# The second layer of an attention-plus-MLP kernel by Strassen's identity, for eight chunks of nine

## The chip, the cores and the metric

The kernel runs on one core of a Trainium2 chip. The metric is the device time of the program in microseconds: before the change the median of three runs is 338.12 us (336.65, 338.12 and 338.40). Five engines work beside each other, each through its own instructions in order: TensorE (PE) with its weight loads (PEld), VectorE (DVE), ScalarE (ACT), GpSimd (POOL), and SyncE (SP), which here only issues transfers. PE writes to PSUM, eight banks of 512 fp32 columns for each of 128 partitions; DVE and ACT carry results from there to SBUF.

## What is computed

Causal attention over 8 batches ("sequences" below) of 8 heads, 576 positions and 64 columns, with 16 beacon keys and values that every query sees, and then an MLP over the 4608 rows of 512 that come out.

```python
def _attn_ref(q, k, v, beacon_k, beacon_v):
    B, H, S, D = q.shape                       # 8, 8, 576, 64
    k_all = np.concatenate([beacon_k, k], axis=2)
    v_all = np.concatenate([beacon_v, v], axis=2)
    ...
    a = np.exp(scores)
    a /= a.sum(-1, keepdims=True) + 1e-09
    return np.matmul(a, v_all)

def _moe_ref(x, w_in, w_out):                  # x 4608x512, w_in 512x2048, w_out 2048x512
    h = x @ w_in
    g = np.maximum(0.01 * h, h)
    return (g @ w_out).astype(np.float32)
```

Inputs and output are fp32; the matmuls take bf16.

## The kernel before

**Attention.** The work goes by pairs of heads, `g` from 0 to 31, four pairs to a sequence. Queries and keys come through POOL's queue, as bf16. For the first eight pairs PE transposes them (`t_q`); for the later ones they are loaded in natural order (`load_natural`, pool `natpool`) and turned by transposing transfers that SP issues (`turn_pair`). Scores go to PSUM; later pairs pack them into blocks of three 1024-column tiles (`stretch`), of which the first takes two buffers of the pool `ps_one` and the others the pool `ps_sc`. ACT takes the exponential into `aT`, POOL sets the masked triangles to zero. `value` multiplies by the values in two halves (12 and 18 matmuls of 65 columns); DVE divides by the row sums (a reciprocal, L380, and a product, L381) and leaves `x_nat`. `x_transposes` (PE and a copy, L398) or `x_turn` (two transposing transfers from SP) put it into `xT`, the activations of all 4608 tokens with model columns on partitions.

**MLP.** Tokens go in nine chunks of 512. `moe1(i, fc)` (an "up") is four matmuls of 512 columns for one of 16 blocks of 128 hidden columns, then a Prelu on ACT (L431) into `gT`, one of two buffers. The second layer ("downs") goes by tiles of 128 tokens: `moe2_part` does 16 matmuls, in four quarters, with `gT` as weights and `w_out_sb` moving, into one PSUM buffer that is held through the four quarters; then DVE copies it to `osb` (L484, two buffers) and SP stores it (L485). Only the very last tile is split into 384 and 128 columns, the latter copied and stored by ACT.

**PSUM.** `ps_sc` has two buffers of two banks. `ps_one` has four buffers of one bank, shared by ups, downs, values, transposes and the first tile of each score block.

**Order.** The order of instructions on all five engines is the program's own. The first eight pairs follow a list of steps written as strings (`run`: `s` scores, `v` values, `u` up, `d` down, `x` finish and so on). Behind it a list of events with due times in units of pairs is walked through; between events `fill` puts in ups and downs so that they are spread evenly over the time. A chunk's ups come as soon as all its tokens are in `xT`, and its downs after all its ups. The last downs stand alone.

SP's queue holds, in order, the transposes of queries and keys, those of `x_nat`, and the output stores. POOL's holds the masks and the loads of q, k and v.

Of the kernel before, what the change touches and what calls it, by code (L numbers as in the profile page):

```python
# [15 lines left out]
def kernel(  # L16
# [11 lines left out]
    nc = tc.nc  # L28
# [31 lines left out]
    NA, NK = 4, 8  # L60
    LAID = 2 * NPAIR
# [15 lines left out]
    qkpool = ctx.enter_context(tc.tile_pool(name="qkpool", bufs=2))  # L77
    natpool = ctx.enter_context(tc.tile_pool(name="natpool", bufs=6))
    headpool = ctx.enter_context(tc.tile_pool(name="headpool", bufs=2))
    gpool = ctx.enter_context(tc.tile_pool(name="gpool", bufs=2))  # L80
    opool = ctx.enter_context(tc.tile_pool(name="opool", bufs=2))
# [10 lines left out]
    w_out_r = moe_w_out.rearrange("(c p e) d -> p c (e d)", p=128, e=2)  # L92

# [4 lines left out]
    xT = singles.tile([128, NJ, NTOK], BF16, name="xT")  # L98
# [5 lines left out]
    first_k = singles.tile([RP, 2, RI, D], FP32, name="first_k")  # L104
    k_nat0 = singles.tile([RP, RI, 2, D], BF16, name="k_nat0")
# [30 lines left out]
    def raw_of(b, grp):  # L136
        if (b, grp) not in qk_raw:
            qk_raw[b, grp] = (
                qkpool.tile([128, 2, RI, D], BF16, name="q_raw"),
                qkpool.tile([128, 2, RI, D], BF16, name="k_raw"),  # L140
            )
        return qk_raw[b, grp]
# [244 lines left out]

    def x_transposes(g, copy):
        b, hp = divmod(g, NPAIR)
        x_nat, _ = xs.pop(g)  # L390
        ps = ps_one.tile([128, 1024], BF16, name="tp", tag="one")
        for t, (q0, rows) in enumerate(QT):
            nc.tensor.transpose(
                ps[:, q0 : q0 + rows],
                x_nat[0:rows, t].rearrange("p e d -> p (e d)"),
                ident[0:rows, 0:rows],
            )
        copy(out=xT[:, hp, b * S : (b + 1) * S], in_=ps[:, 0:S])  # L398

    def x_turn(g):  # L400
        b, hp = divmod(g, NPAIR)
        x_nat, _ = xs.pop(g)
        t1 = NKB if b < B - 1 else NKB - 1
        dst = xT[:, hp, b * S : b * S + 112 + (t1 - 1) * 128]
        nc.sync.dma_start_transpose(
            out=dst[:, 112:].rearrange("c (t r) -> c t r", r=128),
            in_=x_nat[:, 1:t1].rearrange("r t e d -> r (t e d)"),
        )
        if t1 < NKB:
            nc.sync.dma_start_transpose(  # L410
                out=xT[:, hp, NTOK - 80 :], in_=x_nat[0:80, t1].rearrange("r e d -> r (e d)")
            )
        nc.sync.dma_start_transpose(  # L413
            out=dst[:, 0:112], in_=x_nat[0:112, 0].rearrange("r e d -> r (e d)")
        )
# [3 lines left out]
    def moe1(i, fc):  # L419
        if i not in gT:  # L420
            gT[i] = gpool.tile([128, NF, 512], BF16, name="gT")
        acc = ps_one.tile([128, 512], FP32, name="acc", tag="one")
        for j in range(NJ):
            nc.tensor.matmul(  # L424
                out=acc,
                lhsT=w_in_cols(fc, j),
                rhs=xT[:, j, i * 512 : (i + 1) * 512],
                start=(j == 0),
                stop=(j == NJ - 1),
            )  # L430
        nc.scalar.activation(out=gT[i][:, fc, :], in_=acc, func=AF.Prelu, alpha=0.01)  # L431

    early = {}

    def moe1_early(n, j):
        if j == 0:
            early[n] = ps_sc.tile([128, 2, 512], FP32, name="sc", tag="sc")
            if 0 not in gT:
                gT[0] = gpool.tile([128, NF, 512], BF16, name="gT")
        for e in range(2):  # L440
            fc = 2 * n + e
            nc.tensor.matmul(
                out=early[n][:, e],
                lhsT=w_in_cols(fc, j),
                rhs=xT[:, j, 0:512],
                start=(j == 0),
                stop=(j == NJ - 1),
            )
        if j == NJ - 1:
            nc.scalar.activation(  # L450
                out=gT[0][:, 2 * n : 2 * n + 2, :], in_=early[n], func=AF.Prelu, alpha=0.01
            )
            done1[0] += 2

    acc2 = [None]

    def moe2(i, t, quarter):
        t0 = i * 512 + t * 128
        if t0 + 128 < NTOK:
            moe2_part(i, t, quarter, quarter + 1, 0, DM, nc.vector.tensor_copy, nc.sync)  # L460
            return
        n = 3 * DM // 4
        if quarter < 3:
            moe2_part(i, t, 4 * quarter // 3, 4 * (quarter + 1) // 3, 0, n, nc.vector.tensor_copy, nc.sync)
        else:
            moe2_part(i, t, 0, 4, n, DM, nc.scalar.copy, nc.scalar)

    def moe2_part(i, t, q0, q1, lo, hi, copy, eng):
        if q0 == 0:
            acc2[0] = ps_one.tile([128, 512], FP32, name="acc", tag="one")  # L470
        acc = acc2[0][:, 0 : hi - lo]
        for fc in range(q0 * 4, q1 * 4):
            nc.tensor.matmul(  # L473
                out=acc,
                lhsT=gT[i][:, fc, t * 128 : (t + 1) * 128],
                rhs=w_out_sb[:, fc, lo:hi],
                start=(fc == 0),
                stop=(fc == NF - 1),
            )
        if q1 < 4:  # L480
            return
        t0 = i * 512 + t * 128
        osb = opool.tile([128, hi - lo], FP32, name="osb" if lo == 0 and hi == DM else f"osb{lo}")
        copy(out=osb, in_=acc)  # L484
        eng.dma_start(out=out[t0 : t0 + 128, lo:hi], in_=osb)  # L485

    done1, done2, ready, turn, first_down, held = [0], [0], [0], [0], [0], [0]

    def fill():
        i1, fc = divmod(done1[0], NF)  # L490
        i2, n2 = divmod(done2[0], NF)
        can1 = i1 < ready[0] and (i1 < 2 or i2 > i1 - 2)
        can2 = i2 < NCH and i2 < i1 and done1[0] >= first_down[0]
        if held[0] and can2:
            held[0] -= 1
            down()
        elif can1 and (turn[0] == 0 or not can2):
            up()
        elif can2:
            down()  # L500
        return can1 or can2

    def up():
        i1, fc = divmod(done1[0], NF)
        assert i1 < ready[0]
        moe1(i1, fc)
        done1[0] += 1
        turn[0] = 1

    def down():  # L510
        i2, n2 = divmod(done2[0], NF)
        moe2(i2, n2 // 4, n2 % 4)
        done2[0] += 1
        turn[0] = 0
# [40 lines left out]
    def run(steps):  # L555
        for step in steps.split():
# [27 lines left out]
            elif op == "P":  # L584
                moe1_early(*a)
# [8 lines left out]
            elif op == "o":  # L594
                load_w_out(a[0])
            else:
# [12 lines left out]
    with order:  # L609
# [23 lines left out]
        run("m7.1 m7.2 N9.1 u b8.2 b9.2 b10.2 b11.2 x6 v7.0 T9 v7.1 d d d N10.0 N10.1 d V2.0 V2.1 x7 T10")  # L633
# [22 lines left out]
        def has_down():  # L656
            return done2[0] // NF < done1[0] // NF
# [28 lines left out]
        for at, _, what, args in events:  # L686
            while w + 2 < len(ends) and at > ends[w + 1]:
                w, d0 = w + 1, done1[0] + done2[0]
            todo = 2 * NF * ready[0] - KEPT - d0
# [9 lines left out]
        while done2[0] < NCH * NF:  # L699
# [31 lines left out]
```

The softmax here doesn't subtract the row's maximum and nothing guards it: scores larger than these inputs give would overflow.

## Time and profile before

| | |
|---|---|
| Median of the runs | 338.12 us |
| Span of the profiled execution | 339.9 us |
| Mean granted TensorE clock | 0.995 |
| First-layer matmuls (L424), 553 in the trace | 135.9 us busy |
| Second-layer matmuls (L473), 568 in the trace | 131.6 us busy |
| Value matmuls (L351), 960 | 40.0 us busy |
| Masks on POOL (L281), 160 | 57.5 us busy |
| Exponentials of the later pairs (L321 and L325), 128 | 80.6 us busy |
| An output store of 256 KB, from issue to landing | 2.7 us (median) |
| A transposing transfer to `xT`, from issue to landing | 4.3 us (median) |

A group's busy time is the time in which at least one of its instructions runs. Matmuls are pipelined: one shows with about 380 ns though the next begins after some 216, so the distance of starts, and not the length of one, tells what a matmul costs. Some matmul records are missing from the trace (553 of 576, 568 of 592). DMA lines show SP's issue; the landing comes later. In the lines quoted below, what stands behind the bar is the idle time of the engine ahead of such an instruction, and what ended it.

### The profile page before, as it was taken

What the parts mean: (1) busy time and instruction counts of PE and PEld (TensorE: products, weight loads), DVE (VectorE), ACT (ScalarE), POOL (GpSimd) and SP (SyncE); (2) the same over time, 40 slices, a digit from 0 to 9 for tenths busy, and PEclk for the clock granted to TensorE, in tenths of its full rate; (3) what the DMA queues carried; (4) which work ended last, traced back from release to release, by engine and by line L of the source; (5) the groups of instructions that cost most, each with busy time, mean ns of one, the idle gap of its engine ahead of it and who ended that gap; (6) DMA issues with size and microseconds to landing.
All of it is one profiled execution on the core that took longest, in us unless ns stands there. A gap on an engine that the chain in (4) does not pass through costs nothing.

```text
span 339.9 us, 7458 instructions
## 1 busy us (share of the span) xinstructions
PE 328.5 (97%) x2950; PEld 170.7 (50%) x2997; DVE 82.8 (24%) x202; ACT 187.1 (55%) x312; POOL 180.8 (53%) x354
## 2 busy tenths in 40 slices
PE   8989999999996999999999999999999999999996
PEld 5574565455553455544554555545455544444443
DVE  3572354021222112311330232212321220000111
ACT  4969761778554583478536843685368205633300
POOL 8894969968987475668656966675221000000000
PEclk9999999999998999999999999999999999999999
DMA  8999999999999999999999999999211130000012
GB/s 135 129 194 169 149 212 129 177 181 122 163 154 186 160 113 139 137 123 103 110 183 137 112 114 159 159 117 123 89 56 39 23 110 33 0 31 33 31 63 91
DMA packets 151922, 39.84 MB, mean 117 GB/s; under 512 B 143008, under 2 KB 145184, under 8 KB 151888
## 3 DMA queue, kind: packets, MB, share of 16 engines
q0 software_dynamic: 99824, 18.54, 83.0%
q1 hardware_dynamic: 51648, 20.70, 34.0%
q8 instruction: 23, 0.38, 0.5%
q10 hardware_dynamic: 416, 0.13, 0.2%
q14 instruction: 11, 0.09, 0.1%
HBM read 37.22 MB, written 9.44 MB: 137 GB/s over the span
## 4 chain that ended last, share of the span: by engine, by line
PE 82%; DMA 11%; POOL 3%; issue 2%; SPq 0%; DVE 0%; ACT 0%; POOLq 0%; DVEq 0%
PE acc L473 34%; PE acc L424 34%; PE av L351 7%; PE sc L306 5%; DMA v_aug<-in_v_dram 4%; DMA w_in_sb<-in_moe_w_in_dram 4%; DMA out_dram<-osb 3%; POOL aT L281 1%; POOL q_raw L151 1%; POOL k_raw L151 1%; PE sc L259 0%; SPq L413 0%; DVE osb L484 0%; POOL w_in_sb L123 0%; POOL v_aug L206 0%
## 5 line engine op out<-in xcount | busy, mean ns | idle before, releaser
L424 PE MATMUL acc<-xT,w_in_sb 128*128 128x512 bf16 x553 | 135.9, 382 | 4.0 <-DMA xT<-x_nat 1.5
L473 PE MATMUL acc<-w_out_sb,gT 128*128 128x512 bf16 (+2 forms) x568 | 131.6, 373 | 1.5 <-issue 0.2
L431 ACT ACTIVATE gT<-acc 128x512 bf16<-128x512 f32 x144 | 83.8, 618 | 77.3 <-PE acc L424 75.6
L281 POOL TENSOR_SCALAR_AFFINE_SELECT aT<-aT 128x256 bf16<-128x256 bf16 (+2 forms) x160 | 57.5, 388 | 66.8 <-ACT aT L321 40.8
L424 PEld LDWEIGHTS <-w_in_sb 128*128 128x128 bf16 x576 | 53.7, 98 | 66.1 <-issue 8.3
L473 PEld LDWEIGHTS <-gT 128*128 128x128 bf16 x592 | 54.6, 98 | 60.1 <-issue 1.3
L321 ACT ACTIVATE aT<-sc 128x512 bf16<-128x512 f32 (+3 forms) x64 | 28.9, 521 | 49.0 <-PE sc L306 49.0
L325 ACT ACTIVATE aT<-sc 128x1024 bf16<-128x1024 f32 (+3 forms) x64 | 51.7, 893 | 0.0
L484 DVE COPY osb<-acc 128x512 f32<-128x512 f32 (+1 forms) x36 | 24.8, 688 | 96.2 <-PE acc L473 81.8
L380 DVE RECIPROCAL rec<-av 128x6 f32<-128x6 f32 (+1 forms) x64 | 12.1, 188 | 133.7 <-PE av L351 133.5
L351 PEld LDWEIGHTS <-aT 128*128 128x128 bf16 (+1 forms) x960 | 36.6, 98 | 13.5 <-issue 2.4
L351 PE MATMUL av<-v_aug,aT 128*128 128x65 bf16 (+1 forms) x960 | 40.0, 194 | 1.1 <-issue 0.9
L206 POOL DMA_DIRECT2D v_aug<-in_v_dram x40 | 34.1, 857 | 5.1 <-DMA w_in_sb<-in_moe_w_in_dram 4.3
L163 POOL DMA_DIRECT2D q_nat<-in_q_dram x48 | 34.9, 733 | 1.3 <-issue 0.4
L163 POOL DMA_DIRECT2D k_nat<-in_k_dram x48 | 34.8, 732 | 0.4 <-issue 0.3
L381 DVE TENSOR_TENSOR x_nat<-av,rec 128x384 bf16<-128x384 f32 (+1 forms) x64 | 31.4, 491 | 2.2
L268 ACT ACTIVATE aT<-sc 128x1024 bf16<-128x1024 f32 (+3 forms) x32 | 25.9, 875 | 3.3 <-PE sc L259 3.3
L306 PE MATMUL sc<-qT,kT 64*128 64x80 bf16 (+22 forms) x384 | 21.8, 250 | 0.5 <-PE acc L424 0.5
L306 PEld LDWEIGHTS <-kT 64*128 64x128 bf16 x384 | 12.7, 94 | 14.1 <-issue 11.6
L259 PE MATMUL sc<-qT,kT 64*128 64x80 bf16 (+4 forms) x96 | 9.9, 284 | 0.1
L520 PE MATMUL av<-blank 128*128 128x256 bf16 (+2 forms) x41 | 7.8, 349 | 1.1 <-DVE blank L612 1.1
L241 DVE COPY qT<-tp 128x576 bf16<-128x576 bf16 x7 | 5.3, 756 | 12.8 <-PE tp L235 12.8
(44 smaller groups left out, 69.4 us busy)
## 6 DMA issues: line engine op xcount, KB each, us to landing
out_dram<-osb SPq DMA_DIRECT2D x35, 256.0 KB, 2.7
q_nat<-in_q_dram POOLq DMA_DIRECT2D x48, 72.0 KB, 4.7
k_nat<-in_k_dram POOLq DMA_DIRECT2D x48, 72.0 KB, 5.0
v_aug<-in_v_dram POOLq DMA_DIRECT2D x24, 128.0 KB, 6.3
w_in_sb<-in_moe_w_in_dram POOLq DMA_DIRECT2D x2, 1024.0 KB, 12.6
w_out_sb<-in_moe_w_out_dram POOLq DMA_DIRECT2D x2, 1024.0 KB, 11.3
q_raw<-in_q_dram POOLq DMA_DIRECT2D x8, 144.0 KB, 6.8
k_raw<-in_k_dram POOLq DMA_DIRECT2D x7, 144.0 KB, 6.9
```

Of the source, the lines that this page charges most:

```text
L163: nc.gpsimd.dma_start(out=t[:, :, par], in_=(q, k)[which][b, 2 * hp + par].rearrange("(t p) d -> p t d", p=NR),)
L206: nc.gpsimd.dma_start(out=dst[lo : ROWS[c], c, :, 0:D], in_=v[b, :, OFF[c] : OFF[c] + n].rearrange("h p d -> p h d"),)
L268: nc.scalar.activation(out=aT[:, :, c0 : c0 + w], in_=sc[:, :, 0:w], func=AF.Exp, scale=0.125)
L281: nc.gpsimd.affine_select(out=view, in_=view, compare_op=ALU.is_ge, fill=0.0, base=128 - n if lo == 0 else 0, channel_multiplier=-1, patte ...
L306: nc.tensor.matmul(out=(sc[par] if apart else sc[:, par])[:, at : at + b - a], lhsT=kT[ps_, c * 128 : (c + 1) * 128], rhs=qT[ps_, q0 : q0 ...
L321: nc.scalar.activation(out=probs[g][:, par, lo:hi], in_=sc[par][:, at : at + hi - lo], func=AF.Exp, scale=0.125)
L325: nc.scalar.activation(out=probs[g][:, :, lo:hi], in_=sc[:, :, at : at + hi - lo], func=AF.Exp, scale=0.125)
L351: nc.tensor.matmul(out=avv[:, n, 0 : D + 1], lhsT=aT[0 : ROWS[c], par, a0 : a0 + 128], rhs=va[0 : ROWS[c], c, 2 * hp + par, :], start=(c = ...
L381: nc.vector.tensor_tensor(out=x_nat[:, t0:t1].rearrange("p t e d -> p (t e) d"), in0=avv[:, :, 0:D], in1=rec[:, n0:n1, None].to_broadcast( ...
L424: nc.tensor.matmul(out=acc, lhsT=w_in_cols(fc, j), rhs=xT[:, j, i * 512 : (i + 1) * 512], start=(j == 0), stop=(j == NJ - 1),)
L431: nc.scalar.activation(out=gT[i][:, fc, :], in_=acc, func=AF.Prelu, alpha=0.01)
L473: nc.tensor.matmul(out=acc, lhsT=gT[i][:, fc, t * 128 : (t + 1) * 128], rhs=w_out_sb[:, fc, lo:hi], start=(fc == 0), stop=(fc == NF - 1),)
```

## The change

Strassen's identity (in Winograd's form) multiplies two matrices cut into 2 x 2 blocks with seven block products in place of eight, and sums of blocks ahead of and behind them. Here the left matrix is a chunk's `gT`: its 512 tokens are cut in two halves of 256 (A1x and A2x), its 2048 hidden columns in two halves of 1024. The right one is `w_out`, cut into 1024 x 256 blocks. The first chunk keeps the plain form; the other eight take the new one.

- **Weight sums.** Once, in the list of steps (`t0` after the second `d` of the last line, and after the first chunk's last down): three sums of 1024 x 256 (2048 elements per partition) into a new tensor `w_sum`, and one in place in `w_out_sb`. All on DVE.
- **Token sums.** For each Strassen chunk, in two slices of four hidden blocks of each half, four DVE additions of 1024 elements per partition: S1, S2 and S4 into a new tile `gsum`, S3 in place in `gT`. The ups of such a chunk alternate between the halves of the hidden columns, so that a slice is complete after eight ups. A slice's sums are put in behind the next up or ahead of the next down.
- **Products.** In the order 1, 6, 2, 7, 5, 4, 3, each for two tiles of 128 tokens, each with eight matmuls of 256 columns. A "down" is now one tile of one product (8 matmuls); a chunk has 14 of them. Products 1 and 2 add up in one PSUM bank, 7 and 4 in another, 5 and 3 in a third; 6 has one alone. Two are open at a time.
- **Combining.** After product 1 ACT copies the bank to `u2`; after 6 DVE adds it to `u2`; after 2 ACT copies C11 to `osb`; after 7 DVE adds to `u3`; after 5 ACT copies to `p5` and DVE adds that to `u3` (C22); after 4 and 3 DVE adds `u2` to the bank (C21, C12). Each quarter of the output (256 tokens x 256 columns) is stored by SP. In the last chunk products 5 and 3 are combined tile by tile.
- **Room in SBUF.** `xT` becomes a ring of four sequences (2304 columns and 48 for an overhang), so chunk 4, which lies across its end, has its ups in two matmuls of 256 columns each. `natpool` goes from six buffers to four. The raw queries and keys of the first eight pairs, and the first key's buffers, lie in the two `gsum` buffers that the token sums take later. `osb` has three buffers.
- The step `P` (`moe1_early`), which the list doesn't use, is dropped. The pacing counts 14 downs for a Strassen chunk.

```diff
-    natpool = ctx.enter_context(tc.tile_pool(name="natpool", bufs=6))
+    natpool = ctx.enter_context(tc.tile_pool(name="natpool", bufs=4))
+    sumpool = ctx.enter_context(tc.tile_pool(name="sumpool", bufs=2))
...
-    xT = singles.tile([128, NJ, NTOK], BF16, name="xT")
+    xT = singles.tile([128, NJ, XR * S + 48], BF16, name="xT")
...
+    head_k = sumpool.tile([128, 3 * NF // 2 * 256], BF16, name="gsum")
+    head_qk = sumpool.tile([128, 3 * NF // 2 * 256], BF16, name="gsum")
...
+        at = i * 512 % (XR * S)
+        cut = min(512, XR * S - at)
+        for lo, hi in ((0, cut), (cut, 512)):
...
+    def weight_sums(part):
...
+        if part == 0:
+            tt(out=t1, in0=b12, in1=b11, op=SUB)
+            tt(out=t2, in0=b22, in1=t1, op=SUB)
+            tt(out=t4, in0=b21, in1=t2, op=SUB)
+        else:
+            tt(out=b12, in0=b22, in1=b12, op=SUB)
...
+    def token_sums(i, lo, hi):
...
+        tt(out=s1, in0=a21, in1=a22, op=ADD)
+        tt(out=s2, in0=s1, in1=a11, op=SUB)
+        tt(out=a21, in0=a11, in1=a21, op=SUB)
+        tt(out=s4, in0=a12, in1=s2, op=SUB)
...
+    PRODUCTS = (1, 6, 2, 7, 5, 4, 3)
...
+        n, tile = PRODUCTS[n2 // 2], n2 % 2
+        bank = {1: "a", 2: "a", 6: "b", 7: "c", 4: "c", 5: "d", 3: "d"}[n]
+        opens = n in (1, 6, 7, 5)
...
+        for fc in range(HF):
+            nc.tensor.matmul(
+                out=acc[:, lo : lo + HD],
+                lhsT=left(i, n, fc, tile),
+                rhs=right(n, fc),
+                start=(opens and lo == 0 and fc == 0),
+                stop=(fc == HF - 1),
+                skip_group_check=True,
+            )
...
+        if n == 1:
+            nc.scalar.copy(out=kept("u2"), in_=acc)
+        elif n == 6:
+            tt(out=part("u2"), in0=acc, in1=part("u2"), op=ADD)
+        elif n == 2:
+            c = kept("osb", 3)
+            nc.scalar.copy(out=c, in_=acc)
+            store(i, 0, 0, tiles, c)
+        elif n == 7:
+            tt(out=kept("u3"), in0=acc, in1=part("u2"), op=ADD)
+        elif n == 5:
+            c = kept("p5")
+            nc.scalar.copy(out=c, in_=acc)
+            tt(out=part("u3"), in0=part("u3"), in1=c, op=ADD)
+            store(i, 1, 1, tiles, part("u3"))
+        elif n == 4:
+            c = kept("osb", 3)
+            tt(out=c, in0=acc, in1=part("u2"), op=ADD)
+            store(i, 1, 0, tiles, c)
+        elif n == 3:
+            c = kept("osb", 3)
+            tt(out=c, in0=acc, in1=part("u2"), op=ADD)
+            store(i, 0, 1, tiles, c)
...
     def up():
-        i1, fc = divmod(done1[0], NF)
+        i1, n = divmod(done1[0], NF)
         assert i1 < ready[0]
+        fc = n if i1 == 0 else n // 2 + n % 2 * HF
         moe1(i1, fc)
+        add_due()
         done1[0] += 1
         turn[0] = 1
+        if i1 and n % (2 * SLICE) == 2 * SLICE - 1:
+            due.append((i1, n // 2 + 1 - SLICE, n // 2 + 1))
...
-        run("m7.1 m7.2 N9.1 u b8.2 b9.2 b10.2 b11.2 x6 v7.0 T9 v7.1 d d d N10.0 N10.1 d V2.0 V2.1 x7 T10")
+        run("m7.1 m7.2 N9.1 u b8.2 b9.2 b10.2 b11.2 x6 v7.0 T9 v7.1 d d t0 d N10.0 N10.1 d V2.0 V2.1 x7 T10")
```

## The prediction

> **What bounds the kernel now.** First the page: busy shares, the slices, the chain that ended last.
>
> ```profile
> PE 328.5 (97%) x2950; PEld 170.7 (50%) x2997; DVE 82.8 (24%) x202; ACT 187.1 (55%) x312; POOL 180.8 (53%) x354
> PE   8989999999996999999999999999999999999996
> PEclk9999999999998999999999999999999999999999
> PE 82%; DMA 11%; POOL 3%; issue 2%; SPq 0%; DVE 0%; ACT 0%; POOLq 0%; DVEq 0%
> ```
>
> TensorE (PE) is busy in every slice at full clock, but for one dip in the 13th, and holds 82% of the chain. A microsecond of matmul taken away is a microsecond gained, as long as PE then waits for nothing new. So I need the price of a matmul, then what the new VectorE (DVE) and bank waits cost.
>
> The price is read at the end of the timeline, where PE does nothing but the second layer. There a DVE copy starts when a group of 16 matmuls is done, so the distance of two copies is 16 matmuls: columns are start, duration, engine, line.
>
> ```profile
> 329.87 0.69 DVE L484 COPY osb<-acc 128x512 f32<-128x512 f32 x1 [2.76 <-PE acc L473]
> 333.32 0.69 DVE L484 COPY osb<-acc 128x512 f32<-128x512 f32 x1 [2.76 <-PE acc L473]
> 335.92 0.56 DVE L484 COPY osb<-acc 128x384 f32<-128x384 f32 x1 [1.91 <-PE acc L473]
> 336.81 0.27 ACT L484 COPY osb<-acc 128x128 f32<-128x128 f32 x1 [13.26 <-PE acc L473]
> ```
>
> 512 columns: 3.45 us / 16 = 215.6 ns. 384 columns: 2.60 / 16 = 162.5. 128 columns: 0.89 / 16 = 55.6, each with its own weight load. The line through them gives 109 ns for 256 columns; weight loads hide even at 55.6.
>
> Prices for the other engines come from the groups by shape.
>
> ```profile
> L484 DVE COPY osb<-acc 128x512 f32<-128x512 f32 x35 | 24.2, 692 | 94.2 <-PE acc L473 79.9 <-DMA out_dram<-osb 9.3 <-PE sc L306 2.8
> L381 DVE TENSOR_TENSOR x_nat<-av,rec 128x384 bf16<-128x384 f32 x32 | 17.8, 557 | 1.1
> L381 DVE TENSOR_TENSOR x_nat<-av,rec 128x256 bf16<-128x256 f32 x32 | 13.6, 424 | 1.1
> L241 DVE COPY qT<-tp 128x576 bf16<-128x576 bf16 x7 | 5.3, 756 | 12.8 <-PE tp L235 12.8
> L398 DVE COPY xT<-tp 128x576 bf16<-128x576 bf16 x5 | 2.3, 455 | 3.3 <-PE tp L393 3.3
> L431 ACT ACTIVATE gT<-acc 128x512 bf16<-128x512 f32 x144 | 83.8, 618 | 77.3 <-PE acc L424 75.6
> ```
>
> DVE costs 158 ns plus 1.04 ns per element (from 384 and 256 columns). But the bf16 copy with both sides in unbroken runs takes 455 ns for 576 elements, 0.52 ns each, where the strided one takes 756. So DVE has a double rate for packed bf16.
>
> Last, the dip, in the timeline.
>
> ```profile
> 97.82 0.84 PE L306 MATMUL sc<-qT,kT 64*128 64x144 bf16 x16
> 98.31 1.08 ACT L321 ACTIVATE aT<-sc 128x512 bf16<-128x512 f32 x2 [3.12 <-PE sc L306]
> 99.28 2.01 ACT L325 ACTIVATE aT<-sc 128x512 bf16<-128x512 f32 x3
> 101.48 0.69 DVE L484 COPY osb<-acc 128x512 f32<-128x512 f32 x1 [4.59 <-DMA out_dram<-osb]
> 107.93 0.38 PE L424 MATMUL acc<-xT,w_in_sb 128*128 128x512 bf16 x1 [1.53 <-DMA xT<-x_nat]
> 108.57 0.69 DVE L484 COPY osb<-acc 128x512 f32<-128x512 f32 x1 [4.74 <-DMA out_dram<-osb]
> 109.32 0.58 PE L424 MATMUL acc<-xT,w_in_sb 128*128 128x512 bf16 x1 [1.01 <-DVE osb L484]
> 110.13 3.24 PE L424 MATMUL acc<-xT,w_in_sb 128*128 128x512 bf16 x10 [0.22 <-issue]
> ```
>
> DVE twice waits 4.6 us for an old output store (two osb buffers), x_nat queues behind it, the activations come late, PE idles, and in the window from 107 to 112 its granted clock is 0.66. From 105.58 to the next values at 113.21, 16 matmuls took 7.63 us instead of 3.45: 4.2 us lost. The first five lines also show the pattern used below: 16 score matmuls (0.77 us until the next matmul) put 3 us of exponentials into ScalarE (ACT), from 98.31 to 101.29.
>
> **Matmuls: -12.5 us.** A chunk had 64 matmuls of 512 columns: 64 x 215.6 = 13.8 us. It gets 7 products x 2 tiles x 8 = 112 of 256: 112 x 109 = 12.2. Eight chunks: 8 x 1.59 = 12.7 us. The ring of 2304 columns cuts chunk 4 in halves: 128 x 109 for 64 x 215.6, +0.15. Bounds for a 256-column matmul: 107.8 (half of 512) to 111.2 (twice 128), that is -13.8 to -10.7.
>
> **Stores: -3.5 us.** Strassen's outputs use three osb buffers per chunk and one u3, each reused a chunk (some 35 us) later, and the plain chunk's 4 copies also have three. So DVE's two 4.6 us waits should go. SP issues as many stores as before (four a chunk), between the same transposes. Bounds -4.2 to 0; near the upper gain, as only the first chunks crowd SP.
>
> **Token sums.** Per chunk 8 additions of 1024 bf16 elements. No row shows two SBUF sources; at the packed rate 158 + 1024 x 0.52 = 0.69 us, at the other 1.22. All 64 are 44 or 78 us in 340, and DVE is a quarter busy, so only those that PE waits for count. They are the second slice's: product 6 reads S2 right after product 1, and S2 needs the last up's Prelu (0.62 us on ACT) and two additions. Where scores stand just ahead of the last two ups (chunks 2 and 5), with score start as zero: PE ends the ups at 0.77 + 1.73 = 2.5; ACT starts exponentials at 0.49, ends at 3.5, and its two Prelus at 4.7; S2 is there at 4.7 + 1.4 = 6.1 (7.2 at the slow rate). PE reaches fc 4 of product 6 after product 1 (1.74), 12 value matmuls (0.5) and 4 matmuls (0.44): 5.2. So 0.95 (2.0) us late. In the same way the other chunks: 1: 0.8 (1.3), since product 1 itself waits for the second-last Prelu; 3: 0 (0.8); 6: 0 (0.6); 8, in the tail: 0.1 (1.1); 4 and 7: 0. Sum +2.8 (+7.8); nothing excludes 0. I take 2.8: packed, unbroken bf16 is nearest to the 455 ns row. Masks on POOL (0.41 us each) may share a port with these sums: +0.5, between 0 and one mask in each of three chunks, 1.2.
>
> The Trainium skill, "VectorE: DVE Perf Modes", section "Mode 2×_1P", agrees for additions with all operands 16-bit at step one, two results per cycle. Against the change speaks "SBUF — State Buffer", "Who interferes with whom": a VectorE instruction with two SBUF inputs and a GpSimd instruction that reads SBUF exclude each other. By that rule a group of five masks could come between the sums, some 2 us (5 x 0.41) in each of three chunks, an estimate of 6 us for my 0.5; no row here has two SBUF tensors on VectorE.
>
> **Weight sums: +0.8 us.** Three additions of 2048, 1.22 us each (2.29), enter DVE behind the copy at 55.2, and the xT copy, before at 57.2, comes behind them: 55.9 + 3.7 + 0.46 = 60.1 (63.3). PE wants it at 59.60, hence +0.8 with the semaphore; +3.9 at the slow rate. The in-place fourth lies under chunk 1's ups.
>
> **Banks: +1.5 us.** Of four one-bank PSUM buffers Strassen holds two through a chunk where the plain layer held one, and a score block takes two. The matmul group behind such a block (four to five places: values or product 5) must wait for the first exponential, 0.49 + 0.54 us after the block's start, against PE's 0.77: 0.3 to 0.4 us each. Bounds 0 and 3 (twice the places).
>
> **Small things.** Values whose reciprocals queue behind a burst of sums (4 x 0.69): x_nat and banks up to 2.8 us later, mostly covered, as transposes for a coming chunk are issued long before (for the chunk begun at 144.59 the last at 134.53): +0.3 (0 to 2). The last eviction is a DVE sum of 256 columns (0.42) for ACT's 0.27: +0.2. Three ACT copies a chunk, 24 x 0.62 = 15 us, and five DVE combines for four copies lie under matmuls (ACT 55% busy); product 2 waits for product 1's copy, but product 6 (1.74 us) lies between. The smaller pool of naturals (four for six) asks that a load waits for a transpose scheduled three pairs earlier: nothing.
>
> **Sum:** -12.5 - 3.5 + 2.8 + 0.5 + 0.8 + 1.5 + 0.3 + 0.2 = -9.9 us. The profiled span of 339.9 becomes 330.0; the median stands 1.8 below the span: 328.2.
>
> **Rivals.** *Nothing waits* (0.15): ACT and DVE keep ahead, -12.5 - 4.2 + 0.2: 321.6. For it: no PE idle after 112 us before; against: exponentials really sit ahead of the Prelus. *DVE adds one element per cycle* (0.12): the bracketed values, -12.5 - 3.5 + 7.8 + 0.5 + 3.9 + 1.5 + 0.3 + 0.2 = -1.8: 336.3. For it: every two-source row here runs at 1.04 ns; against: those have fp32 sources. *Slower* (0.08): one mechanism, DVE's strict order. Sums wait at DVE's head for Prelus, x_nat waits behind, and transposes miss the next chunk's first matmul, as at 107, with the clock drop: 4.2 us each. Against it the 10 us of lead at 144. From three of the chunk starts on it decides: -9.9 + 12.6 = +2.7, 340.8; five: 349. *It does not save* (0.01): weight loads (98 ns each) bound the 256-column matmul; the 55.6 ns row excludes it.
>
> **Numbers.** The forecast has 0.64. Its own spread, 325 to 332, with parts of the first two rivals gives 323.5 to 334.5. All bounds at once would give -17.8 and +7.4. No change means within 0.5%, 336.4 to 339.8, about what a measurement can tell: 0.06, mostly the one-element rival. Faster 0.85, slower 0.09.
>
> **What would show it.** Second-layer matmuls 109 ns apart; the token sums' row at about 0.69 us; PE waits of about 1 us ahead of products 1 or 6 in chunks 1, 2 and 5; DVE's waits for out_dram gone, and no dip at 107; the first-layer group behind the weight sums waiting for DVE by under 1 us. It is wrong if the sums' row is 1.2 us, or if PE waits for xT at chunk starts.

## The result, and the profile after

The changed kernel takes 349.65 us (median of 4 runs, 348.3 to 350.13), the kernel before beside it 338.26 us (4 runs, 336.65 to 339.07). The ratio is 1.033, with a 95% interval of 1.028 to 1.038: slower by 11.4 us, where 9.9 less was forecast. The profiled execution took 348.3 us, its span is 346.6 us. In this kernel the first pair's queries are overwritten by those of the fifth pair before they are read (shown below); the amount of work is the same.

The page: busy shares, the busy slices of TensorE (PE), its granted clock, the shares of the chain that ended last with the lines it ran through, and the row of the first token sum (S1).

```profile
PE 323.4 (93%) x3429; PEld 214.8 (62%) x3429; DVE 132.9 (38%) x280; ACT 200.4 (58%) x336; POOL 184.8 (53%) x354
PE   5099999999997999999989999999999999999996
PEclk9999999999999999999999999999999999999999
PE 84%; DMA 5%; ACT 4%; DVE 3%; POOL 3%; issue 1%; ACTq 0%; POOLq 0%; SPq 0%
L477 DVE TENSOR_TENSOR gsum<-gT 128x1024 bf16<-128x1024 bf16 x16 | 11.1, 697 | 53.9 <-ACT gT L448 53.9
```

A slice is 346.6 / 40 = 8.7 us. The first has a 5 and the second a 0 where the kernel before had 8 and 9: a hole of about 12 us at the very start, before any Strassen product exists. VectorE (DVE) and ScalarE (ACT) are now in the chain with 3% and 4%, where both had 0%: PE has begun to wait for them. The sum of 1024 elements takes 0.697 us, as forecast (0.69).

The timeline of the changed kernel shows the hole (start, duration, engine, line; in brackets the idle time before and what ended it):

```profile
10.62 0.71 POOL L157 DMA_DIRECT2D gsum<-in_q_dram  x1
17.82 0.69 PE L241 MATMUL tp<-ident,gsum 64*64 64x64 bf16 x18 [11.95 <-DMA gsum<-in_q_dram]
19.04 0.82 PE L643 MATMUL av<-blank 128*128 128x384 bf16 x2
```

The same place in the kernel before:

```profile
5.81 0.60 PE L235 MATMUL tp<-ident,q_raw 64*64 64x64 bf16 x18
6.71 0.50 PE L520 MATMUL av<-blank 128*128 128x384 bf16 x2
11.28 0.62 POOL L151 DMA_DIRECT2D q_raw<-in_q_dram  x1
```

Before, PE transposes the first queries at 5.81, and the load that takes their buffer next is issued behind that, at 11.28. After, that load is issued first (10.62), and the transposes wait 11.95 us for it to land. And when PE starts, two filler matmuls of 384 columns take 0.82 us where they took 0.50: PE runs at about half its rate until 31 us. The granted-clock row shows 9 there all the same; the last section says why it is no witness for these microseconds.

At the other end the new matmuls cost what was forecast. In the tail, where PE does nothing else, two products of 16 matmuls each and the one behind them:

```profile
334.47 3.66 PE L538 MATMUL acc<-w_out_sb,gT 128*128 128x256 bf16 x32
337.96 1.91 PE L538 MATMUL acc<-w_sum,gsum 128*128 128x256 bf16 x16
```

By the distance of starts 32 matmuls of 256 columns take 3.49 us: 109 ns each, the 109 of the forecast.

### The profile page after: what moved, and what is told of

Read it like the earlier page. It is cut to its first block, busy times and chain, and to the rows that moved or that the text cites. A ratio compares the mean times of both kernels' runs of the same rounds, so it can differ in the third digit from the quotient of the medians.

```text
span 346.6 us, 8505 instructions
## 1 busy us (share of the span) xinstructions
PE 323.4 (93%) x3429; PEld 214.8 (62%) x3429; DVE 132.9 (38%) x280; ACT 200.4 (58%) x336; POOL 184.8 (53%) x354
## 4 chain that ended last, share of the span: by engine, by line
PE 84%; DMA 5%; ACT 4%; DVE 3%; POOL 3%; issue 1%; ACTq 0%; POOLq 0%; SPq 0%
PE acc L440 32%; PE acc L538 27%; PE av L357 8%; PE sc L312 5%; PE acc L511 4%; PE sc L265 3%; DMA kT<-k_nat 3%; DMA gsum<-in_q_dram 2%; PE tp L241 2%; ACT aT L331 1%; PE av L643 1%; ACT aT L327 1%; POOL v_aug L212 1%; POOL gsum L157 1%; ACT gT L448 1%
## 5 line engine op out<-in xcount | busy, mean ns | idle before, releaser
L440 PE MATMUL acc<-xT,w_in_sb 128*128 128x512 bf16 (+1 forms) x640 | 135.9, 358 | 0.5 <-DVE x_nat L387 0.3
L448 ACT ACTIVATE gT<-acc 128x512 bf16<-128x512 f32 x144 | 82.9, 620 | 56.4 <-PE acc L440 56.3
L287 POOL TENSOR_SCALAR_AFFINE_SELECT aT<-aT 128x256 bf16<-128x256 bf16 (+2 forms) x160 | 61.1, 406 | 82.1 <-ACT aT L327 36.8
L440 PEld LDWEIGHTS <-w_in_sb 128*128 128x128 bf16 x640 | 59.5, 98 | 53.5 <-issue 3.4
L538 PEld LDWEIGHTS <-gT 128*128 128x128 bf16 x512 | 48.9, 98 | 10.9 <-ACT gT L448 1.9
L538 PE MATMUL acc<-w_out_sb,gT 128*128 128x256 bf16 x384 | 47.1, 273 | 1.3 <-ACT gT L448 1.3
L538 PEld LDWEIGHTS <-gsum 128*128 128x128 bf16 x384 | 36.4, 98 | 6.3 <-DVE gsum L478 0.8
L538 PE MATMUL acc<-w_sum,gsum 128*128 128x256 bf16 x256 | 32.3, 273 | 0.0
L477 DVE TENSOR_TENSOR gsum<-gT 128x1024 bf16<-128x1024 bf16 x16 | 11.1, 697 | 53.9 <-ACT gT L448 53.9
L386 DVE RECIPROCAL rec<-av 128x6 f32<-128x6 f32 (+1 forms) x64 | 11.8, 184 | 51.3 <-PE av L357 51.3
L241 PE MATMUL tp<-ident,gsum 64*64 64x64 bf16 x270 | 7.6, 209 | 11.9 <-DMA gsum<-in_q_dram 11.9
## 6 DMA issues: line engine op xcount, KB each, us to landing
w_out_sb<-in_moe_w_out_dram POOLq DMA_DIRECT2D x2, 1024.0 KB, 12.3
```

The costliest lines, as they stand in the source:

```text
L287: nc.gpsimd.affine_select(out=view, in_=view, compare_op=ALU.is_ge, fill=0.0, base=128 - n if lo == 0 else 0, channel_multiplier=-1, patte ...
L440: nc.tensor.matmul(out=acc[:, lo:hi], lhsT=w_in_cols(fc, j), rhs=xT[:, j, x0 : x0 + hi - lo], start=(j == 0), stop=(j == NJ - 1), skip_gro ...
L538: nc.tensor.matmul(out=acc[:, lo : lo + HD], lhsT=left(i, n, fc, tile), rhs=right(n, fc), start=(opens and lo == 0 and fc == 0), stop=(fc ...
```

## Experiments

### Where the 12 us at the start come from

`raw_of` gives the raw queries and keys of a group of pairs one of two places in one tile, in turn. The third group asked for (the fifth pair's) gets the first's place. Its load stands in program order ahead of the first pair's transposes; a pool with two buffers would have made that load wait for PE, but a fixed slice is only ordered by who is written first. So the transposes come behind the load, and read what it brought. Two experiments take this alone: E1 gives the third group a place of its own in the changed kernel, E2 puts the two fixed places into the kernel before.

E1:

```diff
-            n = len(qk_raw) % 2 * 2
+            t, n = ((head_qk, 0), (head_qk, 2), (head_k, 3), (head_qk, 0))[len(qk_raw)]
             qk_raw[b, grp] = [
-                head_qk[:, m * QK : (m + 1) * QK]...
+                t[:, m * QK : (m + 1) * QK]...
```

> Changed kernel with a third place for the raw queries and keys of the fifth and sixth pair (the free columns behind the first keys), so that their load no longer writes where the first pair's queries lie. Theory A (the load that is issued at 10.6 us overwrites the first pair's place ahead of its transposes, which therefore wait for it): the first transposes come at about 5.8 us as before the change, the 12 us wait and the slow matmuls behind it go, 14.2 us less by the first packed score block, median 335.4 (334 to 337). Rival B (the loads are late because of the shared tile or of the queue, whatever place they write): 349 as in the changed kernel.

Measured: 333.83 us (7 runs), the kernel before 337.73 (17 runs); ratio 0.989 (0.986 to 0.992).

E2 (the first pair's queries are the fifth's here too):

```diff
-    qkpool = ctx.enter_context(tc.tile_pool(name="qkpool", bufs=2))
+    head_qk = singles.tile([128, 4, 2, RI, D], BF16, name="head_qk")
...
-            qk_raw[b, grp] = (
-                qkpool.tile([128, 2, RI, D], BF16, name="q_raw"),
-                qkpool.tile([128, 2, RI, D], BF16, name="k_raw"),
-            )
+            n = len(qk_raw) % 2 * 2
+            qk_raw[b, grp] = [head_qk[:, m] for m in (n, n + 1)]
```

> Kernel before the change, with only this: the raw queries and keys of the first eight pairs lie in one fixed tile with two places taken in turn, instead of a pool of two buffers, as in the changed kernel. The first pair's queries are then read after the fifth pair's have been written there. Theory A: 338.3 + 14 = 352 (349 to 354), first transposes at about 18 us. Rival B (the start is lost to the sharing with the sums' buffers or to the first keys' place): 338.

Measured: 353.96 us; ratio 1.050 (1.045 to 1.055). Its timeline:

```profile
17.70 0.69 PE L233 MATMUL tp<-ident,head_qk 64*64 64x64 bf16 x18 [11.82 <-DMA head_qk<-in_q_dram]
```

Both directions agree: 349.65 - 333.83 = 15.8 us taken away (15.3 if each is held against the kernel before that was measured beside it: 11.4 + 3.9), 353.96 - 337.73 = 16.2 us put on, and the wait is the one of the changed kernel. The placement of the raw queries is the cause, and Strassen has no part in it.

The profiled execution of E1 took 340.0 us with its head at half rate until 24 us although nothing waited, so E1 was run again; the lines of E1 below are from this second profile.

> The kernel with three places for the raw queries and keys once more, for a profile whose start isn't disturbed. Its earlier profiled execution (340.0 us) had its head at half of the matmul rate without any wait, while the median was 333.8. If that was a disturbance of the execution: about 333.8 again, 384-column filler matmuls near 6.7 us at 0.50 us a pair, and the first packed scores near 61 us. If the layout itself slows the head: 0.82 again.

Measured: 334.2 us (10 runs), before 338.53 (13 runs); ratio 0.988 (0.985 to 0.992). Its timeline at the start:

```profile
5.52 0.47 PE L241 MATMUL tp<-ident,gsum 64*64 64x64 bf16 x18 [0.48 <-DMA gsum<-in_q_dram]
6.28 0.50 PE L643 MATMUL av<-blank 128*128 128x384 bf16 x2
```

The wait and the slow matmuls are both gone. From here the 15.8 us can be split: the transposes started 17.82 - 5.52 = 12.3 us late, and the first value matmuls, at 33.08 in the changed kernel's trace and at 16.09 in E1's, 17.0 us late. So 4.7 us are lost behind the wait, where PE runs at half rate; about 1 us is won back until the first packed scores (75.38 against 59.29, 16.1).

### What the layout costs, and what the dip was worth

E6 is E1 with all nine chunks plain, without weight and token sums: what is left of the change is the ring with the halved ups of chunk 4, the smaller `natpool`, three output buffers and the places.

```diff
     def ND(i):
-        return NF if i == 0 else 2 * len(PRODUCTS)
+        return NF if i < NCH else 2 * len(PRODUCTS)
...
-        if i == 0:
+        if i < NCH:
             moe2_plain(i, n2 // 4, n2 % 4)
-            if n2 == NF - 1:
-                weight_sums(1)
             return
...
```

> e1_three_places with all nine chunks in the plain form: no weight sums, no token sums, four tiles of 16 matmuls per chunk; ring, halved ups of chunk 4, four naturals and three output buffers stay. Theory C (Strassen's eight chunks save 12.7 us of matmuls, and lose 9.0 us to waits for banks, sums and Prelus and 0.8 to the weight sums): e1 + 2.9, about 338.3. Rival D (the dip at 107 us of the profiled execution before is in every run, and three output buffers remove it): 338.3 - 4.2 = 334, so that Strassen on its own is a loss of 1 us.

Measured: 338.0 us, ratio 1.000 (0.998 to 1.003). The layout costs nothing once the third place is there, and its third output buffer brings nothing either.

The kernel before was also profiled a second time:

> The kernel before the change once more, for a second profile. If the dip at 107 us was in that one execution only, as its span (339.9) above the median time (338.1) suggests: span about 336.5, no granted clock under 0.9 after 100 us. If it is in every execution: span 339 to 340 and the dip again.

Measured: 336.48 us, span 334.8. The stretch from 107 to 112 us of this second profile (columns: length, then busy time and instructions of PE, weight loads, DVE, ACT and POOL, granted clock, busy DMA engines, GB/s):

```profile
107.00:112.00 5.00, 4.95 (x50) 2.76 (x50) 1.36 (x4) 3.68 (x8) 5.00 (x9) 1.00 1.81 138
```

And of the first, from which the prediction worked:

```profile
107.00:112.00 5.00, 2.83 (x7) 1.08 (x8) 0.69 (x1) 2.48 (x5) 4.84 (x10) 0.66 1.55 225
```

In the second execution PE is busy 4.95 us of 5 at full clock: the dip isn't in every execution. None of the 41 runs of this kernel that were measured beside the experiments has a mean granted clock under 0.998, where the first profiled execution has 0.995. What set it off there is open. A device time here is its span plus 1.7 us (336.48 against 334.8; 348.3 against 346.6), so the first profiled execution, with a span of 339.9, took about 341.6 us, 3.5 more than the median.

### Where 12.5 us of matmuls became 4

E1 gains 3.9 to 4.3 us, not the 12.5 of the matmuls. PE's waits in E1, by what ended them (what waited, what for; us in total, how often, the longest):

```profile
PE sc L312 <- DVE x_nat L387: 2.5, 3, 1.2
PE acc L538 <- ACT gT L448: 2.0, 3, 0.7
PE av L357 <- ACT aT L327: 1.6, 3, 0.8
PE sc L312 <- PE acc L440: 1.2, 2, 0.8
PE av L643 <- DVE blank L735: 1.1, 1, 1.1
...
PE acc L440 <- DVE x_nat L387: 0.3, 1, 0.3
PE acc L440 <- ACT aT L327: 0.2, 1, 0.2
```

In the second profile of the kernel before only two of these kinds appear: 1.1 us for `blank` at the very start, and 0.5 us where scores wait for an up's bank. So 2.5 + 2.0 + 1.6 + 0.7 + 0.3 + 0.2 = 7.3 us are new. The timeline of E1 around the first Strassen chunk shows the largest:

```profile
84.83 0.93 PE L538 MATMUL acc<-w_out_sb,gT 128*128 128x256 bf16 x7
85.69 1.14 ACT L448 ACTIVATE gT<-acc 128x512 bf16<-128x512 f32 x2
86.39 1.16 PE L538 MATMUL acc<-w_out_sb,gT 128*128 128x256 bf16 x9 [0.63 <-ACT gT L448]
86.86 0.78 DVE L477 TENSOR_TENSOR gsum<-gT 128x1024 bf16<-128x1024 bf16 x1 [4.57 <-ACT gT L448]
87.38 1.08 PE L357 MATMUL av<-v_aug,aT 128*128 128x65 bf16 x30
...
88.34 0.88 DVE L479 TENSOR_TENSOR gT<-gT 128x1024 bf16<-128x1024 bf16 x1
...
89.75 0.18 DVE L386 RECIPROCAL rec<-av 128x6 f32<-128x6 f32 x1
89.97 0.56 DVE L387 TENSOR_TENSOR x_nat<-av,rec 128x384 bf16<-128x384 f32 x1
...
90.58 0.18 PE L312 MATMUL sc<-qT,kT 64*128 64x16 bf16 x1 [1.24 <-DVE x_nat L387]
...
91.64 1.09 ACT L327 ACTIVATE aT<-sc 128x512 bf16<-128x512 f32 x2 [3.47 <-PE sc L312]
...
92.28 0.65 PE L357 MATMUL av<-v_aug,aT 128*128 128x65 bf16 x12 [0.30 <-ACT aT L327]
```

At 86.39 product 1 waits for the last Prelu. The distance of starts gives a little more than the bracket: 7 matmuls of 109 ns from 84.83 end at 85.59, so 0.80 us, not 0.63; ends of matmuls are modelled, so the waits of the view are lower bounds. At 87.38 PE begins the values, 30 matmuls in 1.08 us. Their division stands in DVE's order behind four token sums, of which the first had waited 4.57 us for that same Prelu, and runs from 89.75. Until it is done the values hold two banks of `ps_one`, product 1 (whose bank stays open for product 2) and product 6 hold two more, and the score block at 90.58, which needs two, waits. At 92.28 the next values wait for a bank that the block's first exponential gives back.

The waits cost more than their own length in this execution (the last row has the columns of the stretch from 107 to 112 us above, the granted clock third from the end):

```profile
88.31 1.04 PE L538 MATMUL acc<-w_sum,gsum 128*128 128x256 bf16 x8
92.74 1.90 PE L538 MATMUL acc<-w_sum,gsum 128*128 128x256 bf16 x8
92.50:96.00 3.50, 3.50 (x27) 2.58 (x24) 1.44 (x3) 2.12 (x4) 2.59 (x7) 0.51 1.82 99
```

Right behind them the granted clock is 0.51 for 3.5 us, and eight matmuls that took 1.04 us take 1.90: some 1.7 us, which no wait lists. Five of the ten runs of this second E1 have a mean granted clock of 0.994, with a median of 335.4 us; the other five have 0.999 or 1.000, with 333.07.

So there are two candidates for the waits: the sums in DVE's order, and the banks that the products hold. Six runs bear on them.

E4 doubles the burst: the sums of a chunk in one slice.

```diff
-    SLICE = 4
+    SLICE = 8
```

> e1_three_places with the token sums of a chunk in one burst behind its last up: four additions of 2048 elements in place of two bursts of four with 1024. Theory S (DVE's burst between the last Prelu and product 6 sets the start of a chunk's products, and holds values' banks meanwhile): an addition takes about 1.22 us, S2 comes 1.1 us later and is wanted 0.44 us earlier, so up to 1.5 us in each of the chunks 1, 2, 3, 5, 6 and 8, and the two waits for x_nat grow by 2.1 us each: +6 to +12, 340 to 346. Rival (DVE has room, as it is 39% busy): 334, as e1.

Measured: 345.59 us, ratio 1.022 (1.017 to 1.028), 11.8 us more than E1. Its timeline:

```profile
90.61 1.05 PE L538 MATMUL acc<-w_sum,gsum 128*128 128x256 bf16 x8 [1.07 <-DVE gsum L478]
93.78 0.18 PE L312 MATMUL sc<-qT,kT 64*128 64x16 bf16 x1 [2.13 <-DVE x_nat L387]
```

and of its waits the longest:

```profile
PE acc L538 <- DVE gsum L478: 7.9, 7, 1.5
```

Now product 6 waits for S2 as well, which it never did in E1, 7.9 us in seven places, and the score block's wait grows from 1.24 to 2.13 us (the score blocks' waits for `x_nat` from 2.5 to 4.3). Behind two of these places the granted clock is 0.50 for 3.4 us. So most of the 11.8 us is S2 coming late, which costs E1 nothing: E4 shows that PE does wait for DVE's burst once it is longer, and doesn't tell the two candidates apart.

E7 keeps E1's two slices but puts S3 and S4, which only products 7 and 3 read, in four steps later.

```diff
+        if not late:
+            tt(out=s1, in0=a21, in1=a22, op=ADD)
+            tt(out=s2, in0=s1, in1=a11, op=SUB)
+            return
         tt(out=a21, in0=a11, in1=a21, op=SUB)
         tt(out=s4, in0=a12, in1=s2, op=SUB)
...
+            due.append([1, i1, n // 2 + 1 - SLICE, n // 2 + 1, False])
+            due.append([LATE, i1, n // 2 + 1 - SLICE, n // 2 + 1, True])
```

> e1_three_places with S3 and S4 of each slice put in four calls later (for the second slice ahead of product 2), so that the divisions of values come first. Theory X (score blocks wait for a bank that a value holds whose division stands behind S3 and S4: 1.41 + 0.54 us at the first, 1.03 at the fourth Strassen chunk): each shrinks by up to the 1.37 us of the two additions, -2 to -3: 331 to 332. Rival (the bank is late for another reason, the products holding two): within 1 of e1's 333.8.

Measured: 330.99 us, ratio 0.979 (0.975 to 0.984). The same score block in its timeline, and the values and their division ahead of it:

```profile
88.53 1.08 PE L357 MATMUL av<-v_aug,aT 128*128 128x65 bf16 x30
89.70 0.56 DVE L387 TENSOR_TENSOR x_nat<-av,rec 128x384 bf16<-128x384 f32 x1
90.42 0.18 PE L312 MATMUL sc<-qT,kT 64*128 64x16 bf16 x1
90.86 0.85 PE L312 MATMUL sc<-qT,kT 64*128 64x16 bf16 x15 [0.26 <-DVE x_nat L387]
```

The division follows the start of the values by 1.2 us, where in E1 it was 2.6 (87.38 and 89.97), and the score block begins without a wait.

E11 leaves the 64 token sums out of E1 altogether (the products read `gT` in their place, so the output is another):

```diff
-            token_sums(*due.pop(0))
+            due.pop(0)
...
-        return sums[i][:, {5: 0, 6: 1, 3: 2}[n], fc, t]
+        return gT[i][:, fc, t]
```

> The three-places kernel without the 64 token sums: products 5, 6 and 3 read gT where they read the sums, so the output isn't the reference's; all matmuls, copies and combines stay. My theory: of the PE waits that I read in the changed kernel (9.0 us), those for Prelus at product 1 (2.45) and about 0.35 us at each of the four score blocks that share the banks (1.4, the wait for the first exponential alone) stay, and the rest, some 4.7 us, is x_nat behind the sums in DVE's order and goes: 333.8 - 4.7 = 329.1. Rival 1, the banks held by the products are the cause and not DVE's order: only masks and the like go, 333.3. Rival 2, by the prediction's own sizes (2.8 for token sums, 0.5 for the masks): the token-sum term goes but for the Prelu waits, 333.8 - 0.9 = 332.9.

Measured: 331.36 us, ratio 0.978 (0.971 to 0.985), 2.8 us below E1. In its waits those for `x_nat` are gone, and those for the first exponential are what they were:

```profile
PE av L357 <- ACT aT L327: 1.6, 3, 0.8
...
PE acc L538 <- ACT gT L448: 0.7, 1, 0.7
```

So the sums cost some 2.8 us in E1, and E7 gets as much by moving half of them. It isn't the 4.7 that I expected. I had counted part of the exponentials' waits to the sums, which belong to the banks. E11's profile also lists 2.3 us of waits for `kT` at three score blocks, which E1's doesn't; but this execution took 335.41 us, 4 more than the median, with its head at half rate until 24 us, so they may not be in the others, and the rest of the difference stays open.

E8 is E1 with the other remedy. Each product has a bank of its own that is opened and given back with it, and the combining takes one bank at a time.

```diff
-    PRODUCTS = (1, 6, 2, 7, 5, 4, 3)
+    PRODUCTS = (1, 2, 6, 7, 5, 4, 3)
...
-        if opens and (tile == 0 or apart):
-            banks[bank, tile] = ps_one.tile([128, 512], FP32, name="acc", tag="one")
+        if tile == 0 or apart:
+            banks["p"] = ps_one.tile([128, 512], FP32, name="acc", tag="one")
...
-                start=(opens and lo == 0 and fc == 0),
+                start=(lo == 0 and fc == 0),
...
         elif n == 2:
             c = kept("osb", 3)
-            nc.scalar.copy(out=c, in_=acc)
+            tt(out=c, in0=acc, in1=part("u2"), op=ADD)
...
         elif n == 5:
-            c = kept("p5")
-            nc.scalar.copy(out=c, in_=acc)
-            tt(out=part("u3"), in0=part("u3"), in1=c, op=ADD)
+            tt(out=kept("u4"), in0=acc, in1=part("u2"), op=ADD)
+            c = kept("osb", 3)
+            tt(out=c, in0=acc, in1=part("u3"), op=ADD)
...
```

> e1_three_places with every product in a bank of its own that is given back after it: order 1, 2, 6, 7, 5, 4, 3, no adding up of two products in PSUM; product 1 is copied by ACT, the others are added by DVE (2, 6 to product 1's copy; 7 and 5 to u2; 5 and 4 to u3; 3 to u4). Per chunk two ACT copies fewer, two DVE additions out of PSUM more (8 x 2 x 0.69 = 11 us on DVE). Theory B (two banks held through a chunk cause the waits of score blocks and values: 0.35 + 1.41 + 0.54 + 0.53 + 0.55 + 1.03 + 0.67 + 1.0 = 6.1 us): 327.7 to 330; the waits for Prelus (0.79, 0.83, 0.83) stay. Rival (DVE is the one that holds banks; more DVE work makes it worse): 334 to 337.

Measured: 329.62 us, ratio 0.977 (0.972 to 0.981). Its waits:

```profile
PE acc L536 <- ACT gT L448: 2.0, 3, 0.7
PE sc L312 <- PE acc L440: 1.2, 2, 0.8
PE sc L312 <- DVE x_nat L387: 1.1, 1, 1.1
...
PE av L357 <- DVE x_nat L387: 0.2, 1, 0.2
```

The 1.6 us for exponentials ahead of values are no longer listed, those for `x_nat` ahead of scores and values are down from 2.5 to 1.3, although E8 leaves the sums where they were and gives DVE more work (142.9 us busy against 132.9 in E1). E8 also changes the order of the products and has two ACT copies a chunk fewer (ACT 190.6 us busy for 199.7), and no run takes these apart from the bank. The waits for Prelus, which an emptier ACT would shorten first, stay at 2.0 us, and S2, which the new order reads later, was never late in E1; so the free bank is the likely cause, by argument. E12 takes the sums out of E8 in the same way as E11 does, and E9 is E8 with E7's delay:

> The one-bank kernel without the 64 token sums, same omission. If one free bank more already takes away what the sums cost through DVE's order: within 0.6 us of the one-bank kernel's 329.6 (the masks' 16 ns each and little else). If the sums still cost there by their waits: 327 to 328.

> e8_one_bank and e7_late_s3_s4 together. Theories B and X together: no bank waits left, e8 or up to 1 us below: 327 to 329.5. If only X holds: as e7; if only B: as e8.

Measured: E12 329.53 us, ratio 0.974 (0.969 to 0.980); E9 329.88, ratio 0.978 (0.972 to 0.983). In this layout neither moving the sums nor leaving them out brings anything that can be told (329.62, 329.88, 329.53), and my expectation for E9, 327 to 329.5, is missed. E8's 1.3 us of waits for `x_nat` are gone in both profiles, but a wait for `xT` at a chunk start stands in their place:

```profile
106.69 2.97 PE L440 MATMUL acc<-xT,w_in_sb 128*128 128x512 bf16 x13 [1.45 <-DMA xT<-x_nat]
```

This is from E9's timeline; E12, without sums, has 1.52 us of it at 107.69. So beside the Prelus at product 1 (2.0 us in E9) what PE waits for next is the transposing transfer to `xT`. That a version with earlier transfers would gain those 1.3 us wasn't tried.

E8 beats both kernels: 2.3% below the one before, 20 us below the changed one.

## Why the prediction was wrong

**The failed step is one that the prediction doesn't have: it put no price on the move of the raw queries and keys into two fixed places.** Under "Small things" it went through the smaller pool of naturals, whose loads do wait for a buffer, and ended with "nothing"; the raw ones had gone from a pool to a slice taken in turn, and nothing was asked about them. The question left out was which load now stands ahead of which reader: that of the fifth pair stands ahead of the first transposes, and goes into the same place. The runs show a wait of 11.95 us and PE at half its rate behind it, +15 to +16 us (15.3 by E1 and 16.2 by E2, each against the kernel before beside it), more than any term that was priced and of the other sign than the sum.

Without this step the sum would still have promised too much: E1, the kernel that the prediction had in mind, gains 3.9 to 4.3 us and not 9.9. The other terms, held against E1:

- **Matmuls, -12.5: right.** 109 ns in the tail, as forecast; the balance with E1's waits is below.
- **Stores, -3.5: nothing of it in the median.** The dip was in the profiled execution and not in the second one, and E6, with three output buffers, measures 1.000. The sign was there: the profiled execution's span was above the median of the runs, though a run's time is its span plus 1.7 us. The prediction noted "the median stands 1.8 below the span" and took it as an offset instead of asking what was slow in that execution. So a loss that the median doesn't contain was taken off it.
- **Token sums, +2.8: near in size, by luck in part.** Double rate as foreseen (0.697 us). But 1.9 of the 2.8 were S2 late for product 6 in two chunks, and S2 is never late; what PE does wait for is the Prelu at product 1, foreseen for one chunk with 0.8 us and found in three with 2.0 us together.
- **Banks, +1.5: about right**, 1.6 us of values waiting for the first exponential (three places, 0.3 to 0.8, for four or five of 0.3 to 0.4).
- **Small things, +0.3 for divisions queued behind a burst of sums: mis-sized.** 2.5 us in E1's waits, 2.8 by E11 against E1. "Mostly covered" was argued for `x_nat` as input of a coming chunk, which had its 10 us of lead; the banks, which the same sentence names, had no such lead. With two held by the products, what is late behind the division is the next score block. The rival "slower" had the mechanism, DVE's strict order, but put it at chunk starts.
- **Masks and the port, +0.5:** small in sum, as foreseen, though the two do get in each other's way. The 96 masks of 256 columns, in the groups of the changed kernel:

```profile
L287 POOL TENSOR_SCALAR_AFFINE_SELECT aT<-aT 128x256 bf16<-128x256 bf16 x96 | 39.9, 426 | 64.6 <-ACT aT L327 33.9 <-ACT aT L331 18.4 <-ACT aT L274 8.8
```

  In E11, without the sums, the mean is 411. But this mean is over masks that mostly have no sum beside them. The masks beside the first Strassen chunk's sums in E1 (shortest, median and longest, in ns):

```profile
L287 POOL TENSOR_SCALAR_AFFINE_SELECT aT<-aT x5: 345/438/847, 86.0 to 87.8; 128x256 bf16<-128x256 bf16 x3, 80x160 bf16<-80x160 bf16 x1, 128x224 bf16<-128x224 bf16 x1
```

  In E1's whole trace only 8 of 160 masks run beside a sum; they take 0.73 us on average and up to 0.85, the others 0.39. The sums that meet them take up to 0.89 us for 0.69. The Trainium skill's rule that two such instructions exclude each other ("SBUF — State Buffer", "Who interferes with whom") fits these rows: a mask that meets sums takes twice its time. The prediction's estimate of 6 us by it was too high: only these few meet. How much of it reaches PE wasn't tried apart from the sums.
- **Weight sums, +0.8:** scores there wait 0.8 us where the second profile of before has 0.5: about +0.3. The first-layer group behind the weight sums, which was to wait for DVE, doesn't.

The balance: -12.5 and 7.3 us of new waits make -5.2; E1 measures -3.9 and -4.3. The rest, about a us, isn't settled: the waits' view falls short (0.63 for 0.80 above), and half of the second E1's runs lost some clock behind the waits. For the changed kernel, with the 16.2 us of E2, which has no Strassen in it, 338.3 - 4.1 + 16.2 = 350.4, against 349.65 measured.

## What to carry to other kernels

When a buffer moves from a rotating pool to a fixed slice, walk through the program in order for each load into it: the pool made the load wait for the last reader, and a slice makes the reader wait for the load if that stands first. Before a dip in one profile is counted as gain, compare that execution with the median of the runs. And when an in-order engine gets new bursts, ask not only who reads its next result but who waits for the buffers that its next instruction frees; the version that frees a PSUM bank (E8, with the products in another order) was worth as much here as moving the bursts, and the two together no more.

## What was not expected of the hardware

After the 12 us wait PE ran at half its rate (0.82 us for what takes 0.50) from 17.82 to about 31 us, although it was busy all that time. It cost 4.7 us, over a third of the wait on top of it. The granted-clock row shows full speed there, but it says nothing: the trace's first clock record of this execution is at 30.80 us, and time without a record counts as full. The profile of E2, with the same wait, has the records. Its columns as above, the granted clock third from the end:

```profile
5.90:9.30 3.40, 0.00 (x0) 0.00 (x0) 0.00 (x0) 0.00 (x0) 3.40 (x6) 1.00 1.46 151
9.30:17.70 8.40, 0.00 (x1) 0.00 (x1) 0.00 (x0) 0.00 (x0) 3.42 (x5) 0.50 1.87 156
17.70:29.80 12.10, 12.10 (x140) 5.46 (x140) 3.85 (x6) 7.61 (x9) 3.17 (x9) 0.50 0.34 65
29.80:40.00 10.20, 10.20 (x244) 7.84 (x243) 6.66 (x18) 7.67 (x10) 8.32 (x19) 1.00 0.73 113
```

The clock falls to half 3.4 us after PE's last matmul has ended (5.88) and stays there for 12.1 us after PE is busy again. The changed kernel's other three runs have a mean granted clock of 0.965 or 0.966, so they lost it too. The Trainium skill tells of such a state ("TensorE: Matmul & The Clock Gate", "Part 1: The HAM clock gate"): half the clock after an idle window of about 3.4 us. The rows agree on the rate and on the fall; but by the page one busy window of the same length ends it, and here it lasted 12 to 13 us. What ended it no run here shows. E1's first profile and E11's were at half rate from their first matmul until 24 us without any wait, so a late rise to full rate isn't the wait's doing alone.
